# The end of an attention stage: score memory closed a round earlier, feed-forward loads issued from there, products regrouped

## The chip, the cores and the metric

The kernel runs on one core of a Trainium2 chip. The metric is the device time of one execution in microseconds (us), as the median over runs. Lower is better. The core has five engines that each work through their own list of instructions in order and wait for one another by semaphores: TensorE (PE, matmuls; PEld is its weight load), VectorE (DVE), ScalarE (ACT), GpSimd (POOL) and SyncE (SP), which here only issues transfers (DMA).

## The reference

Two stages follow each other: attention with a logarithmic position bias, and a feed-forward network with softplus.

```python
# attention: B, H, S, D = 4, 8, 576, 64
scores = scale * np.matmul(q, k.transpose(0, 1, 3, 2))
scores = scores + bias.transpose(2, 0, 1)[None, :, :, :]
scores = scores - np.max(scores, axis=-1, keepdims=True)
attn = np.exp(scores)
attn = attn / (np.sum(attn, axis=-1, keepdims=True) + 1e-09)
attn_out = np.matmul(attn, v)
# feed-forward: 2304 tokens, d_model 512, d_ff 2048
x = np.ascontiguousarray(attn_out.transpose(0, 2, 1, 3)).reshape(B * S, H * D)
h = x @ w_in
g = np.maximum(h, 0.0) + np.log1p(np.exp(-np.abs(h)))
return (g @ w_out).astype(np.float32)
```

Inputs of the weights are 64-bit floats, which the kernel turns into 32-bit ones with integer operations (`bits`, five steps, the tokens B below) and stores in device memory (`w_d`).

## The kernel before

Attention goes in 16 rounds, n = 0 to 15, each for one batch and one pair of heads. The order of the work in a round is written out by hand as a string of tokens; `emit` turns each into instructions, and each engine keeps the order in which its instructions are emitted. In round n the scores of round n+1 are made beside the second half of round n:

- S, A, X: a score tile of round n+1: its matmuls (line 336), the addition of the bias with the row's extreme (354, DVE), and the exponential (372, ACT).
- T*jc*/buffer: transposes (401) of three tiles of probabilities into a buffer of PSUM (`s0`, `s1`, `t` as 0, 1, 2, or the free half of the output's own memory, `o`); V*jc*/a or /d: the copy out of it into `pt` on ACT (305) or DVE (307). The buffer is free for the next T after its V.
- P0 to P4: the product of `pt` with the values (460), five column blocks that accumulate into `o`. P3 and P4 of round n stand in round n+1.
- I, R, C, G: the reciprocal of the row sums (498, 499), its transpose, the copy and its transfer out (514, 515), and the broadcast loads `rb` (521). O: `o` times `rb` gives `x` (480), which frees `o`; Y: four transfers of `x` to `x_d` (486 to 489).
- B0 to B4, W: `bits` of one weight tile and the store to `w_d` (695).
- D: transposes of the identity matrix whose result nobody reads (629).

Round 15 has no scores to make. Before it the memory for scores (`es_s`: q, k, the bias tiles and, in PSUM, `s0` and `s1`) is closed (line 958) and the pools of the feed-forward stage take its place, among them four PSUM banks for `h`. SP's list then gets three loads of `x` and two of weights (960 to 962). Transposes of round 15 use `t` and `o` alone. The tokens f0 to f12 (`FIRST`) put the first work of the feed-forward stage between them: `wl` loads a weight tile, `xl` loads `x`; `w` (741 on ACT, 743 on POOL or DVE) and `x` (759 on ACT, 760 on DVE) split a tile into a rounded part and the remainder, and `step`.

`step(i)` (line 908) emits, for one visit (512 tokens by 128 of d_ff): `emit_h` (772, 12 matmuls), the softplus of the visit before (`emit_g`, 788 to 804), the splitting of the weights of the visit after (`w_fin`), and `emit_y` (830) of the visit three before. There are 80 visits. Step 0 and 1 are emitted inside round 15, those from 2 on behind it.

```python
 958             es_s.close()
 959             open_ffn()
 960             x_load(0, range(3))
 961             w_load(0, 0)
 962             w_load(1, 0)
```

Of the kernel before, what the change touches and what calls it, by code (L numbers as in the profile page):

```python
# [9 lines left out]
F32 = mybir.dt.float32  # L10
# [6 lines left out]
PSUM = bass.MemoryType.PSUM  # L17
# [11 lines left out]
SH = S // 2  # L29
# [15 lines left out]
ROUND = """  # L45
# [2 lines left out]
G S7/0 S6/2 L4 A8 V20/a T22/1 T11/2 V41/a b V31/d T30/0 B2 A7 b X3 V11/a V22/a b P0 V30/d A5 A6 L1  # L48
X7 P1 X8 B3 X6 X5 L2 P2 T32/0 V32/d L3 B4 W
"""  # L50
STEADY = range(2, 15)
SETS = ((2, 4), (3, 8), (7, 5, 6), (1, 0))

ROUND0 = """
# [6 lines left out]
ROUND1 = """  # L61
# [3 lines left out]
X6 L3 P2 B4 X5 L2  # L65
"""

ROUND15 = """
P3 T00/2 D4 I P4 V00/a T02/2 D4 V02/a T10/2 D6 O R/o V10/a C T01/o V01/d T32/2 V32/d T11/o T12/2 f2 V11/a
V12/a T22/o V22/d f4 P0 T21/2 f3 V21/a f0 P1 T20/2 V20/a f7 T30/2 V30/a T40/2 f8 f1 V40/a f9 B0  # L70
f11 T41/2 P2 B1 f5 f10 V41/a f6 T31/2 B2 B3 f12 V31/a B4
"""
ROUND16 = """
P3 P4 O
"""

FIRST = (
    ('x', 0, 1), ('wl', 0, 1), ('w', 0, 0, True), ('x', 0, 0), ('xl', 0, (3,)), ('wl', 2, 0),
    ('wl', 1, 1), ('x', 0, 2), ('w', 1, 0, True), ('x', 0, 3), ('w', 0, 1, True), ('step', 0), ('step', 1),
)  # L80
FIRST_STEP = 2

PLACE = (0, 1, 2, 3, 4, 7, 8, 5, 6)
# [32 lines left out]
def tile_log_bias_attention__then__softplus_ffn(  # L116
# [13 lines left out]
    nc = tc.nc  # L130
# [9 lines left out]
    def pool(es, name, bufs, side="left", space=SB):  # L140
        return es.enter_context(
            tc.tile_pool(name=name, bufs=bufs, side=side, space=space, reuse_waits="tile")
        )

    const = ctx.enter_context(tc.tile_pool(name="const", bufs=1))
    ident = const.tile([128, 128], F32, name="ident")
# [6 lines left out]
    es_s = ctx.enter_context(ExitStack())  # L153
    nat = pool(es_s, "nat", NAT, "right")
    bp = pool(es_s, "bp", 18, "right")
    ps_s = pool(es_s, "ps_s", 1, "right", PSUM)
    s_buf = [ps_s.tile([128, 2, 512], F32, name=f"s{i}") for i in range(2)]

    es_p = ctx.enter_context(ExitStack())
# [95 lines left out]
    N = 16  # L255
# [123 lines left out]
    def tail(n, i):  # L379

        assert all(("e", n, t) in done for t in TAILS[i])
        done.add(("l", n, i))
        tl = pp.tile([128, 2, 64], F32, tag="tl", name="tl", bufs=9)
        if i < 4:
            src = pairs.pop((n, i))[:, :, 512:S]
        else:
            src = prob[n, 4][:, 512:S].rearrange("p (o c) -> p o c", o=1)
            src = src.to_broadcast([128, 2, 64])
        nc.gpsimd.tensor_copy(tl, src)
        tails[n, i] = tl.rearrange("p a c -> p (a c)")  # L390

    s_use, s_held = [0], set()
    spare = {}

    def turn(blocks, on=None):
        ps = ps_o if on == "o" else s_buf[int(on)]
# [171 lines left out]
    def emit(n, tok):  # L568

        tok, _, on = tok.partition("/")  # L570
        on = (on,) if on else ()
        kind, late_ = tok.rstrip("0123456789"), tok[len(tok.rstrip("0123456789")):]
        a = [int(c) for c in late_]

        def stage(key, make, i, *arg):
            if key not in units:
                units[key] = make(*key[1:])
            units[key][i](*arg)

        if kind in ("S", "A", "X"):  # L580
            if n + 1 < N:
                stage(("s", n + 1, *a), u_s, "SAX".index(kind), *on)
        elif kind in ("Z", "ZA", "ZX"):
            stage(("s", n, *a), u_s, ("Z", "ZA", "ZX").index(kind))
        elif kind == "L":
            if n + 1 < N:
                tail(n + 1, *a)
        elif kind == "ZL":
            tail(n, *a)
        elif kind in ("T", "V"):  # L590
            stage(("t", n, *a), u_t, "TV".index(kind), *on)
        elif kind == "P":
            stage(("p", n - (a[0] >= PV_LATE), *a), u_pv, 0)
        elif kind == "I":
            inv(n)
        elif kind in ("R", "C"):
            stage(("r", n), u_r, "RC".index(kind), *on)
        elif kind == "O":
            if n:
                stage(("x", n - 1), u_x, 0)  # L600
                if n not in STEADY:
                    defer(8, lambda: stage(("x", n - 1), u_x, 1))
        elif kind == "B":
            if 1 <= n <= len(pre):
                stage(("b", n - 1), u_bits, *a)
                if a[0] == 4 and n not in STEADY:
                    defer(8, lambda: stage(("b", n - 1), u_bits, 5))
        elif kind in ("k", "q"):
            emit_load(n + 3, kind)
        elif kind == "v":  # L610
            emit_load_v(n + 2)
        elif kind == "w":
            pre_load(n)
        elif kind == "b":
            if tiles:
                emit_bias(*tiles.pop(0))
        elif kind == "G":
            units["r", n][2]()
        elif kind == "Y":
            stage(("x", n - 1), u_x, 1)  # L620
        elif kind == "W":
            if 1 <= n <= len(pre):
                stage(("b", n - 1), u_bits, 5)
        elif kind == "D":
            if n == N - 1 and "h" not in spare:
                spare["h"] = fp["h"].tile([128, 512], F32, tag="h", name="h")
            to = spare["h"][:, 0:128] if n == N - 1 else ps_o[:, 0, SH:SH + 128]
            for _ in range(a[0]):
                nc.tensor.transpose(to, ident, ident)
        elif kind == "f":  # L630
            w, *arg = FIRST[int(late_)]
            FFN[w](*arg)
        else:
            assert False, tok
# [3 lines left out]
    def defer(k, f):  # L638
        waiting.append([k, f])
# [45 lines left out]
    pre = PRE  # L685
# [3 lines left out]
    def pre_load(i):  # L689
        if i < len(pre):  # L690
            raws[i] = load_raw(dec, *pre[i])
# [6 lines left out]
    es_f = ctx.enter_context(ExitStack())  # L698
    fp = {}

    def open_ffn():
        for nm, bufs in (("raw2", 4), ("xr", 3), ("x0", 4), ("ew", 2), ("gp", 2), ("wr", 1)):
            fp[nm] = pool(es_f, nm, bufs, "right")
        fp["h"] = pool(es_f, "ps_h", 4, "right", PSUM)

    NF = DFF // 128
    wi, wo, wraw = {}, {}, {}
# [2 lines left out]
    def w_load(f, i):  # L710
        if (f, i) in slot:
            a = fp["raw2"].tile([128, 512], F32, tag="a", name="a")
            nc.sync.dma_start(out=a, in_=w_d[slot[f, i]])
        else:
            a = load_raw(fp["raw"], f, i)
        wraw[f, i] = a
# [31 lines left out]
    def x_load(bi, cs=range(4)):  # L748
        t0, nb = blocks[bi]
        for c in cs:  # L750
            a = fp["xr"].tile([128, 512], F32, tag="xr", name="xr")
            nc.sync.dma_start(out=a[:, :nb], in_=x_d[c, :, t0:t0 + nb])
            xraw[bi, c] = a
# [9 lines left out]
    hs, gs, ys = {}, {}, {}  # L763
    def emit_h(bi, f):
        nb = blocks[bi][1]
        ps = spare.pop("h", None)
        if ps is None:
            ps = fp["h"].tile([128, 512], F32, tag="h", name="h")
        i = 0
        for c in range(4):  # L770
            for a, x_ in ((0, 0), (0, 1), (1, 0)):
                nc.tensor.matmul(  # L772
                    ps[:, :nb],
                    lhsT=wi[f][:, a, 128 * c:128 * c + 128],
                    rhs=xs[bi, c][:, x_, :nb],
                    start=(i == 0),
                    stop=(i == 11),
                )
                i += 1
        hs[bi, f] = ps  # L780
# [105 lines left out]
    ps_t, ps_o = (ps_a.tile([128, 2, 512], F32, name=nm) for nm in ("t", "o"))  # L886
# [66 lines left out]
        "step": step,  # L953
    }
    for n in range(N + 1):
        if n == N - 1:
            assert not s_held
            es_s.close()
            open_ffn()
            x_load(0, range(3))  # L960
            w_load(0, 0)
            w_load(1, 0)
        tiles = [(n // B + 1 + (n % B == 3), t) for t in SETS[n % B]]
        if n < 3:
            tiles = [(1, t) for t in ((), range(5), range(5, 9))[n]]
        if n == 1:
            assert not s_held
            s_use[0] = 0
        toks = {0: ROUND0, 1: ROUND1, N - 1: ROUND15, N: ROUND16}.get(n, ROUND).split()
        for i, tok in enumerate(toks):  # L970
            load = {0: LOADS0, 1: LOADS}.get(n, LOADS if n > N - 2 else {}).get(i)
            if load in ("k", "q"):
                emit_load(n + 3, load)
            elif load == "v":
                emit_load_v(n + 2)
            elif load == "v1":
# [93 lines left out]
```

## Time and profile before

| | us |
|---|---|
| median of 3 runs | 685.0 (683.39 to 686.06) |
| the profiled execution, its own time | 685.62 |
| its span, first to last instruction | 683.8 |
| PE busy in the span | 648.1 (95%) |
| ACT, DVE busy | 513.8 (75%), 497.2 (73%) |
| chain that ended last: PE's share | 88% |

In the page, the second part shows busy tenths in 40 slices of 17.1 us. From the seventh slice to the 39th PE stands at 9, except for a 7 in the 16th (256 to 274 us), and in the 16th and 17th PEclk reads 8: that is the end of attention. The windows of the trace, which give each engine's busy time and the granted TensorE clock in any stretch (1.00 is 2.4 GHz, 0.50 is 1.2 GHz), show the place closely. The timeline by engine lists what ran when, with the idle time ahead of it and what ended that in square brackets; the chain gives the steps that set the end.

### The profile page before, as it was taken

What the parts mean: (1) busy time and instruction counts of PE and PEld (TensorE: products, weight loads), DVE (VectorE), ACT (ScalarE), POOL (GpSimd) and SP (SyncE); (2) the same over time, 40 slices, a digit from 0 to 9 for tenths busy, and PEclk for the clock granted to TensorE, in tenths of its full rate; (3) what the DMA queues carried; (4) which work ended last, traced back from release to release, by engine and by line L of the source; (5) the groups of instructions that cost most, each with busy time, mean ns of one, the idle gap of its engine ahead of it and who ended that gap; (6) DMA issues with size and microseconds to landing.
All of it is one profiled execution on the core that took longest, in us unless ns stands there. A gap on an engine that the chain in (4) does not pass through costs nothing.

```text
span 683.8 us, 13233 instructions
## 1 busy us (share of the span) xinstructions
PE 648.1 (95%) x4821; PEld 482.4 (71%) x4821; DVE 497.2 (73%) x1079; ACT 513.8 (75%) x1061; POOL 37.3 (5%) x106
## 2 busy tenths in 40 slices
PE   5688879999999997999999999999999999999997
PEld 2123447667666674678888888888888888888886
DVE  6996558999999994589696874696775565555564
ACT  5899659999999994778686776786676665665654
POOL 0000111111111111100000000000000000000000
PEclk9999989999999998899999999999999999999999
DMA  4986938889788634462240303320300221302220
GB/s 141 310 287 210 343 119 275 265 249 291 247 270 269 196 124 137 131 193 87 99 147 32 115 9 109 107 93 32 106 19 0 108 78 67 119 0 85 70 93 32
DMA packets 51041, 96.85 MB, mean 142 GB/s; under 512 B 7440, under 2 KB 19104, under 8 KB 50976
## 3 DMA queue, kind: packets, MB, share of 16 engines
q1 hardware_dynamic: 50208, 95.34, 42.2%
q8 instruction: 38, 0.62, 0.4%
q10 hardware_dynamic: 768, 0.66, 0.3%
q14 instruction: 27, 0.22, 0.1%
HBM read 67.98 MB, written 28.01 MB: 140 GB/s over the span
## 4 chain that ended last, share of the span: by engine, by line
PE 88%; ACT 5%; DMA 4%; DVE 1%; issue 1%; SPq 1%; ACTq 0%; DVEq 0%
PE y L830 29%; PE h L772 28%; PE o L460 11%; PE s L336 6%; PE s L401 4%; PE t L336 3%; PE acc L225 3%; PE t L401 2%; DMA e_d<-e 2%; ACT e L246 1%; ACT p L372 1%; PE o L401 1%; PE o L336 1%; DMA rb<-r_d 1%; DMA dist<-in_c_dist_dram 1%
## 5 line engine op out<-in xcount | busy, mean ns | idle before, releaser
L772 PE MATMUL h<-x,wi 128*128 128x512 f32 (+1 forms) x960 | 213.8, 372 | 0.3 <-DVE wi L743 0.3
L830 PE MATMUL y<-wo,g 128*128 128x512 f32 x864 | 209.8, 391 | 0.0
L772 PEld LDWEIGHTS h<-x,wi 128*128 128x128 f32 x960 | 170.4, 190 | 33.9 <-DVE wi L743 0.7
L830 PEld LDWEIGHTS y<-wo,g 128*128 128x128 f32 x864 | 161.2, 188 | 33.7 <-DVE g L804 0.2
L795 DVE SCALAR_TENSOR_TENSOR u<-u,e 128x512 f32<-128x512 f32 (+1 forms) x80 | 50.9, 637 | 105.4 <-ACT l L792 105.0
L372 ACT ACTIVATE p<-p,m 128x576 f32<-128x576 f32 x144 | 110.4, 769 | 5.4 <-DVE m L354 1.8
L788 ACT ACTIVATE e<-h 128x512 f32<-128x512 f32 (+1 forms) x80 | 44.3, 553 | 76.7 <-PE h L772 76.7
L460 PE MATMUL o<-pt,vn 128*64 128x256 f32 (+3 forms) x640 | 85.4, 427 | 0.8 <-DVE pt L307 0.7
L354 DVE CUSTOM_DVE_ANT_0 p<-s,b 128x576 f32<-128x576 f32 x79 | 58.4, 753 | 8.5 <-ACT e L246 3.4
L802 ACT ACTIVATE g<-l 128x512 fp32r<-128x512 f32 (+1 forms) x80 | 46.8, 585 | 20.2 <-DVE l L799 10.6
L336 PE MATMUL s<-kn,qn 64*128 64x288 f32 (+1 forms) x416 | 58.6, 415 | 0.2 <-ACT p L347 0.2
L460 PEld LDWEIGHTS o<-pt,vn 128*64 128x64 f32 (+1 forms) x640 | 37.9, 139 | 29.3 <-issue 9.5
L804 DVE TENSOR_TENSOR g<-l,g 128x512 fp32r<-128x512 f32 (+1 forms) x80 | 50.3, 628 | 3.7 <-ACT g L802 3.7
L225 PE MATMUL acc<-m,coef 128*32 128x512 f32 (+17 forms) x352 | 35.5, 502 | 16.4 <-ACT e L246 8.6
L799 DVE TENSOR_TENSOR l<-l,u 128x512 f32<-128x512 f32 (+1 forms) x80 | 50.4, 630 | 0.0
L797 DVE SCALAR_TENSOR_TENSOR l<-h,l 128x512 f32<-128x512 f32 (+1 forms) x80 | 50.4, 630 | 0.0
L792 ACT ACTIVATE l<-u 128x512 f32<-128x512 f32 (+1 forms) x80 | 47.1, 589 | 2.9
L789 ACT ACTIVATE e<-e 128x512 f32<-128x512 f32 (+1 forms) x80 | 47.2, 590 | 2.6
L791 ACT ACTIVATE u<-e 128x512 f32<-128x512 f32 (+1 forms) x80 | 47.2, 590 | 2.5
L305 ACT ACTIVATE pt<-s 128x384 f32<-128x384 f32 x88 | 42.0, 484 | 6.3 <-ACT r L514 4.5
L212 DVE TENSOR_SCALAR m<-lw,pb 128x576 f32<-128x576 f32 (+17 forms) x122 | 44.2, 445 | 0.0
L401 PEld LDWEIGHTS s<-ident,p 64*128 64x128 f32 x624 | 30.7, 142 | 15.6 <-DVE m L354 6.4
(73 smaller groups left out, 692.3 us busy)
## 6 DMA issues: line engine op xcount, KB each, us to landing
e_d<-e SPq DMA_DIRECT2D x36, 295.5 KB, 3.4
qn<-in_q_dram SPq DMA_DIRECT2D x16, 576.0 KB, 6.4
b<-e_d SPq DMA_DIRECT2D x32, 288.0 KB, 3.9
r<-in_moe_w_in_dram SPq DMA_DIRECT2D x16, 512.0 KB, 3.8
r<-in_moe_w_out_dram SPq DMA_DIRECT2D x16, 512.0 KB, 4.3
xr<-x_d SPq DMA_DIRECT2D x28, 256.0 KB, 4.0
vn<-in_v_dram SPq DMA_DIRECT2D x16, 320.0 KB
kn<-in_k_dram SPq DMA_DIRECT2D x16, 288.0 KB, 6.6
```

What stands on the lines that cost most here:

```text
L225: nc.tensor.matmul(acc[32 * g:32 * g + 32, lo:hi], lhsT=coef.rearrange("p o h -> p (o h)"), rhs=hid[s, g][:, lo:hi], start=True, stop=True ...
L336: nc.tensor.matmul(ps[at:at + w, half, :SH], lhsT=q_n[n][rows, hd, c0:c0 + w], rhs=k_n[n][rows, hd], start=True, stop=True, tile_position= ...
L354: nc.vector.tensor_tensor_reduce(prob[n, t].rearrange("p (a c) -> p a c", a=2), st_["ps"], bias[pr, t].rearrange("p (a c) -> p a c", a=2), ...
L372: nc.scalar.activation(p, p, AF.Exp, bias=st_["m"], scale=-1.0, accum_out=ssum[n][:, PLACE.index(t):PLACE.index(t) + 1],)
L401: nc.tensor.transpose(ps[:, a, i], src[rows], ident[rows, 64 * a:64 * a + 64], tile_position=(64 * a, 0))
L460: nc.tensor.matmul(o[up, half, 0:w], lhsT=v_n[n][rows, jb, hd], rhs=pt[n, jb][rows, c0:c0 + w], start=(jb == 0), stop=(jb == 4), tile_posi ...
L772: nc.tensor.matmul(ps[:, :nb], lhsT=wi[f][:, a, 128 * c:128 * c + 128], rhs=xs[bi, c][:, x_, :nb], start=(i == 0), stop=(i == 11),)
L795: nc.vector.scalar_tensor_tensor(u, u, -1.0, e, op0=ALU.add, op1=ALU.subtract)
L797: nc.vector.scalar_tensor_tensor(l, ps, 0.0, l, op0=ALU.max, op1=ALU.add)
L799: nc.vector.tensor_tensor(l, l, u, op=ALU.subtract)
L804: nc.vector.tensor_tensor(g[:, 1], l, g[:, 0], op=ALU.subtract)
L830: nc.tensor.matmul(y, lhsT=g[:, a, 128 * ts:128 * ts + 128], rhs=wo[f][:, w_], start=(first and i == 0), stop=(last and i == 2),)
```

## The change

The memory for scores is closed in two parts. Its SBUF part (q, k, bias) closes inside round 14, by a new token E behind the last bias addition (A6), and the feed-forward pools open there; `h`'s PSUM pool no longer does. Tokens f0 to f2 right behind E load weight tile 0, all four parts of `x` (a pool with four buffers now) and weight tile 1. The buffers `s0` and `s1` stay open until a new token F in round 16, and `h` opens there. Round 15 thus transposes into three buffers, has no D, keeps P3 and P4 of round 14 together and P0, P1, P2 together, and does its roundings (f6 to f11: `w` of tile 0, `x` four times, `w` of tile 1) behind most copies. Round 16 does P3, P4, then step 0, the last O, and step 1. The store of the weight bits of round 14 (W) moves behind the new loads. The tables' rows are cut.

```diff
-STEADY = range(2, 15)
+STEADY = range(2, 17)
+ROUND14 = """
...
+G S7/0 S6/2 L4 A8 V20/a T22/1 T11/2 V41/a b V31/d T30/0 B2 A7 b X3 V11/a V22/a b P0 V30/d A5 A6 E f0
+f1 f2 L1 X7 P1 X8 B3 X6 X5 L2 P2 T32/0 V32/d L3 B4
+"""
 ROUND16 = """
-P3 P4 O
+P3 P4 F f13 O Y B1 B2 B3 B4 f14 W1
 """
 FIRST = (
-    ('x', 0, 1), ('wl', 0, 1), ('w', 0, 0, True), ('x', 0, 0), ('xl', 0, (3,)), ('wl', 2, 0),
...
+    ('wl', 0, 0), ('xl', 0), ('wl', 1, 0), ('wl', 0, 1), ('wl', 2, 0), ('wl', 1, 1),
+    ('w', 0, 0, True), ('x', 0, 0), ('x', 0, 1), ('x', 0, 2), ('x', 0, 3), ('w', 1, 0, True), ('w', 0, 1, True),
+    ('step', 0), ('step', 1),
 )
@@
-    ps_s = pool(es_s, "ps_s", 1, "right", PSUM)
+    es_u = ctx.enter_context(ExitStack())
+    ps_s = pool(es_u, "ps_s", 1, "right", PSUM)
@@
         elif kind == "B":
-            if 1 <= n <= len(pre):
-                stage(("b", n - 1), u_bits, *a)
+            i = min(n, N - 1) - 1
+            if 0 <= i < len(pre):
+                stage(("b", i), u_bits, *a)
@@
         elif kind == "W":
-            if 1 <= n <= len(pre):
-                stage(("b", n - 1), u_bits, 5)
+            i = n - 1 - (a[0] if a else 0)
+            if 0 <= i < len(pre):
+                stage(("b", i), u_bits, 5)
@@
+        elif kind == "E":
+            assert not s_held
+            es_s.close()
+            open_ffn()
+        elif kind == "F":
+            es_u.close()
+            fp["h"] = pool(es_f, "ps_h", 4, "right", PSUM)
@@
-        for nm, bufs in (("raw2", 4), ("xr", 3), ("x0", 4), ("ew", 2), ("gp", 2), ("wr", 1)):
+        for nm, bufs in (("raw2", 4), ("xr", 4), ("x0", 4), ("ew", 2), ("gp", 2), ("wr", 1)):
@@
-        if n == N - 1:
-            assert not s_held
-            es_s.close()
-            open_ffn()
-            x_load(0, range(3))
-            w_load(0, 0)
-            w_load(1, 0)
@@
-        toks = {0: ROUND0, 1: ROUND1, N - 1: ROUND15, N: ROUND16}.get(n, ROUND).split()
+        toks = {0: ROUND0, 1: ROUND1, N - 2: ROUND14, N - 1: ROUND15, N: ROUND16}.get(n, ROUND).split()
```

SP's list at the change of rounds 14 and 15, before (`a` is a weight tile's buffer, `xr` one of `x`; the first three of the rows behind the store are `x`):

```order
L695 DMA w_d_61<-a_3996 128x512
L752 DMA xr_4208<-x_d_59 128x512
L752 DMA xr_4210<-x_d_59 128x512
L752 DMA xr_4212<-x_d_59 128x512
L713 DMA a_4214<-w_d_61 128x512
L713 DMA a_4216<-w_d_61 128x512
L486 DMA x_d_59<-x_4265 128x256
L487 DMA x_d_59<-x_4265 64x320
L488 DMA x_d_59<-x_4265 64x256
L489 DMA x_d_59<-x_4265 64x64
L752 DMA xr_4318<-x_d_59 128x512
```

The same place of SP's list now:

```order
L727 DMA a_4176<-w_d_61 128x512
L766 DMA xr_4178<-x_d_59 128x512
L766 DMA xr_4180<-x_d_59 128x512
L766 DMA xr_4182<-x_d_59 128x512
L766 DMA xr_4184<-x_d_59 128x512
L727 DMA a_4186<-w_d_61 128x512
L710 DMA w_d_61<-a_3996 128x512
L727 DMA a_4276<-w_d_61 128x512
L495 DMA x_d_59<-x_4284 128x256
L496 DMA x_d_59<-x_4284 64x320
L497 DMA x_d_59<-x_4284 64x256
L498 DMA x_d_59<-x_4284 64x64
```

The six loads moved ahead of the store, and the first weight tile ahead of `x`.

ACT's list in round 15, before, from the copy of the row sums on (`wi0`, `wi1` are the weight tiles' rounded parts):

```order
L514 ACTIVATE r_4271<-o_876 9x128
L515 DMA r_d_60<-r_4271 9x128
L741 ACTIVATE wi0_4305<-a_4214 128x512
L305 ACTIVATE pt_4252<-o_876 128x2x3x64
L305 ACTIVATE pt_4252<-t_875 128x2x3x64
L759 ACTIVATE x_4330<-xr_4208 128x512
L305 ACTIVATE pt_4310<-t_875 128x2x3x64
L759 ACTIVATE x_4334<-xr_4210 128x512
L305 ACTIVATE pt_4310<-t_875 128x2x3x64
L759 ACTIVATE x_4348<-xr_4212 128x512
L305 ACTIVATE pt_4281<-t_875 128x2x3x64
L741 ACTIVATE wi1_4367<-a_4216 128x512
```

ACT's list in round 15 now, from behind the same copy and its transfer:

```order
L315 ACTIVATE pt_4224<-s0_82 128x2x3x64
L315 ACTIVATE pt_4215<-s1_83 128x2x3x64
L315 ACTIVATE pt_4231<-t_875 128x2x3x64
L315 ACTIVATE pt_4314<-s1_83 128x2x3x64
L315 ACTIVATE pt_4314<-t_875 128x2x3x64
L755 ACTIVATE wi0_4340<-a_4176 128x512
L773 ACTIVATE x_4343<-xr_4178 128x512
L773 ACTIVATE x_4350<-xr_4180 128x512
L773 ACTIVATE x_4353<-xr_4182 128x512
L773 ACTIVATE x_4360<-xr_4184 128x512
L755 ACTIVATE wi1_4363<-a_4186 128x512
L315 ACTIVATE pt_4366<-s1_83 128x2x2x64
```

The roundings that stood between the copies now stand in one piece behind five of them and ahead of one.

PE's list at the first `h`, before (`tl` are the last 64 columns of the probabilities, T40 and T41):

```order
L401 MATMUL t_875<-ident_66,tl_4104 128x64 x2
L401 MATMUL t_875<-ident_66,tl_4156 128x64 x2
L772 MATMUL h_4229<-x_4330,wi0_4305 128x512 x3
L772 MATMUL h_4229<-x_4334,wi0_4305 128x512 x3
L772 MATMUL h_4229<-x_4348,wi0_4305 128x512 x3
L772 MATMUL h_4229<-x_4373,wi0_4305 128x512 x3
L401 MATMUL t_875<-ident_66,tl_4116 128x64 x2
L401 MATMUL t_875<-ident_66,tl_4167 128x64 x2
L401 MATMUL t_875<-ident_66,tl_4180 128x64 x2
L460 MATMUL o_876<-pt_4310,vn_3804 64x256 x2
L460 MATMUL o_876<-pt_4310,vn_3804 64x320 x2
```

PE's list at the same place now:

```order
L410 MATMUL s1_83<-ident_66,tl_4104 128x64 x2
L410 MATMUL s1_83<-ident_66,tl_4188 128x64 x2
L410 MATMUL s0_82<-ident_66,tl_4116 128x64 x2
L410 MATMUL s0_82<-ident_66,tl_4199 128x64 x2
L410 MATMUL s0_82<-ident_66,tl_4212 128x64 x2
L469 MATMUL o_876<-pt_4314,vn_3804 64x256 x2
L469 MATMUL o_876<-pt_4314,vn_3804 64x320 x2
L469 MATMUL o_876<-pt_4366,vn_3804 64x256 x2
L469 MATMUL o_876<-pt_4366,vn_3804 64x320 x2
L784 MATMUL h_4397<-x_4343,wi0_4340 128x512 x3
L784 MATMUL h_4397<-x_4350,wi0_4340 128x512 x3
```

All transposes and products of attention now stand ahead of the first `h`.

## Rows read from the trace of the kernel before

**Rows 1.** Windows: stretch, its length, each engine's busy us, granted clock, DMA share

```profile
259.40:268.30 8.90, 7.44 (x82) 4.46 (x80) 3.60 (x9) 3.10 (x8) 0.54 (x2) 1.00 0.65 190
268.30:275.20 6.90, 4.57 (x26) 2.33 (x28) 1.35 (x3) 2.92 (x6) 1.27 (x1) 0.51 0.33 106
275.20:278.60 3.40, 2.14 (x23) 1.34 (x20) 1.19 (x2) 2.56 (x6) 0.49 (x1) 1.00 0.70 239
278.60:282.00 3.40, 3.40 (x10) 2.65 (x9) 2.49 (x3) 1.42 (x3) 2.87 (x3) 0.50 0.30 80
282.00:295.40 13.40, 13.14 (x76) 8.70 (x75) 9.38 (x17) 11.55 (x21) 0.00 (x0) 1.00 0.45 139
295.40:683.80 388.40, 384.81 (x1776) 320.31 (x1775) 260.85 (x461) 264.51 (x469) 0.00 (x0) 1.00 0.22 76
```

**Rows 2.** Timeline of PE: start, duration, what, idle time before and its releaser

```profile
256.29 3.13 PE L460 MATMUL o<-pt,vn 128*64 128x256 f32 x24
...
262.44 0.77 PE L460 MATMUL o<-pt,vn 64*64 64x256 f32 x8
...
269.91 0.58 PE L401 MATMUL o<-ident,p 64*128 64x64 f32 x6 [2.03 <-ACT pt L305]
271.22 2.19 PE L460 MATMUL o<-pt,vn 128*64 128x256 f32 x8 [0.72 <-DVE pt L307]
...
287.20 1.89 PE L460 MATMUL o<-pt,vn 128*64 128x256 f32 x16
...
292.80 2.59 PE L772 MATMUL h<-x,wi 128*128 128x512 f32 x10 [0.26 <-DVE wi L743]
295.23 1.09 PE L830 MATMUL y<-wo,g 128*128 128x512 f32 x4
```

**Rows 3.** Timeline of SP's queue at the change of rounds 14 and 15

```profile
255.58 1.82 SPq L521 DMA_DIRECT2D rb<-r_d  x3
260.98 0.33 SPq L695 DMA_DIRECT2D w_d<-a  x1
261.40 2.47 SPq L752 DMA_DIRECT2D xr<-x_d  x3
263.92 0.91 SPq L713 DMA_DIRECT2D a<-w_d  x2
```

**Rows 4.** Timeline of ACT in rounds 14 and 15 and the first steps

```profile
260.57 0.19 ACT L372 ACTIVATION_READ_ACCUMULATOR p<-p,m 128x1 f32 x1
...
268.85 0.63 ACT L741 ACTIVATE wi<-a 128x512 fp32r<-128x512 f32 x1 [3.01 <-DMA a<-w_d]
269.39 0.47 ACT L305 ACTIVATE pt<-o 128x384 f32<-128x384 f32 x1
269.76 0.48 ACT L305 ACTIVATE pt<-t 128x384 f32<-128x384 f32 x1
...
283.30 0.59 ACT L788 ACTIVATE e<-h 128x512 f32<-128x512 f32 x1
...
287.31 0.60 ACT L788 ACTIVATE e<-h 128x512 f32<-128x512 f32 x1
```

**Rows 5.** Timeline of DVE at the same places

```profile
258.33 0.76 DVE L354 CUSTOM_DVE_ANT_0 p<-t,b 128x576 f32<-128x576 f32 x1
...
261.06 0.21 DVE L499 RECIPROCAL ss<-ss 128x9 f32<-128x9 f32 x1
263.25 0.82 DVE L480 TENSOR_TENSOR x<-o,rb 128x256 f32<-128x256 f32 x2 [1.97 <-PE o L460]
...
287.12 0.68 DVE L743 TENSOR_TENSOR wi<-a,wi 128x512 fp32r<-128x512 f32 x1
...
292.06 0.68 DVE L743 TENSOR_TENSOR wi<-a,wi 128x512 fp32r<-128x512 f32 x1
```

**Rows 6.** Windows of the transposes alone (line 401), at attention's start; granted clock fourth

```profile
70.00:73.15 3.15, 2.73 (x46) 0.56 0.93 339
...
73.80:76.00 2.20, 0.40 (x6) 1.00 1.04 390
```

More of the change, by code (lines that the diff above doesn't have):

```diff
@@ L66 @@
 """
+ROUND14 = """
+T10/2 I T00/1 S2/2 S1/1 V10/a B0 S0/0 w T21/0 R/2 A1 C v P3 P4 q A0 V00/a S4/1 A2 B1 X1 k X0 O T40/1
+S3/2 T12/o V21/a A4 V40/d X2 T01/2 Y T02/0 S8/o S5/1 V02/a V01/d b T41/0 T20/1 V12/a X4 T31/o L0 A3
+G S7/0 S6/2 L4 A8 V20/a T22/1 T11/2 V41/a b V31/d T30/0 B2 A7 b X3 V11/a V22/a b P0 V30/d A5 A6 E f0
+f1 f2 L1 X7 P1 X8 B3 X6 X5 L2 P2 T32/0 V32/d L3 B4
+"""
 ROUND15 = """
-P3 T00/2 D4 I P4 V00/a T02/2 D4 V02/a T10/2 D6 O R/o V10/a C T01/o V01/d T32/2 V32/d T11/o T12/2 f2 V11/a
-V12/a T22/o V22/d f4 P0 T21/2 f3 V21/a f0 P1 T20/2 V20/a f7 T30/2 V30/a T40/2 f8 f1 V40/a f9 B0
-f11 T41/2 P2 B1 f5 f10 V41/a f6 T31/2 B2 B3 f12 V31/a B4
+T10/2 I T00/1 T21/0 V10/a V00/d R/2 V21/a C T20/1 V20/d P3 P4 T01/0 V01/a W1 T02/2 V02/d f3 T11/1 O
+V11/a Y T12/0 V12/d T22/2 V22/a G f4 f5 T30/1 V30/a T31/0 V31/d T32/2 V32/a P0 f6 f7 P1 f8 f9 P2 f10
+f11 T40/1 V40/a T41/0 V41/d B0 f12
 """
 ROUND16 = """
-P3 P4 O
+P3 P4 F f13 O Y B1 B2 B3 B4 f14 W1
 """
 FIRST = (
-    ('x', 0, 1), ('wl', 0, 1), ('w', 0, 0, True), ('x', 0, 0), ('xl', 0, (3,)), ('wl', 2, 0),
-    ('wl', 1, 1), ('x', 0, 2), ('w', 1, 0, True), ('x', 0, 3), ('w', 0, 1, True), ('step', 0), ('step', 1),
+    ('wl', 0, 0), ('xl', 0), ('wl', 1, 0), ('wl', 0, 1), ('wl', 2, 0), ('wl', 1, 1),
+    ('w', 0, 0, True), ('x', 0, 0), ('x', 0, 1), ('x', 0, 2), ('x', 0, 3), ('w', 1, 0, True), ('w', 0, 1, True),
+    ('step', 0), ('step', 1),
 )
@@ L392, in tile_log_bias_attention__then__softplus_ffn @@
     s_use, s_held = [0], set()
-    spare = {}
     def turn(blocks, on=None):
@@ L621, in emit @@
         elif kind == "W":
-            if 1 <= n <= len(pre):
-                stage(("b", n - 1), u_bits, 5)
+            i = n - 1 - (a[0] if a else 0)
+            if 0 <= i < len(pre):
+                stage(("b", i), u_bits, 5)
         elif kind == "D":
-            if n == N - 1 and "h" not in spare:
-                spare["h"] = fp["h"].tile([128, 512], F32, tag="h", name="h")
-            to = spare["h"][:, 0:128] if n == N - 1 else ps_o[:, 0, SH:SH + 128]
             for _ in range(a[0]):
-                nc.tensor.transpose(to, ident, ident)
+                nc.tensor.transpose(ps_o[:, 0, SH:SH + 128], ident, ident)
+        elif kind == "E":
[5 more added lines that the diff above has]
+            fp["h"] = pool(es_f, "ps_h", 4, "right", PSUM)
         elif kind == "f":
@@ L701, in open_ffn @@
     def open_ffn():
-        for nm, bufs in (("raw2", 4), ("xr", 3), ("x0", 4), ("ew", 2), ("gp", 2), ("wr", 1)):
+        for nm, bufs in (("raw2", 4), ("xr", 4), ("x0", 4), ("ew", 2), ("gp", 2), ("wr", 1)):
             fp[nm] = pool(es_f, nm, bufs, "right")
-        fp["h"] = pool(es_f, "ps_h", 4, "right", PSUM)
     NF = DFF // 128
@@ L765, in emit_h @@
         nb = blocks[bi][1]
-        ps = spare.pop("h", None)
-        if ps is None:
-            ps = fp["h"].tile([128, 512], F32, tag="h", name="h")
+        ps = fp["h"].tile([128, 512], F32, tag="h", name="h")
         i = 0
```

## The prediction

> **What bounds the kernel now.** I read the windows first. From 295.40 us to the end PE is busy 384.81 of 388.40 us at full clock [rows 1]: that is the feed-forward stage, bound by PE, and the change touches nothing in it. Its 1776 matmuls, 192 of them half as wide, make 1680 full ones, so one costs 388.40 / 1680 = 0.231 us and an `h` of twelve 2.77 us. What can move is the stretch from 259.40, when round 14's P0 to P2 end [rows 2], to the first `y` at 295.23 [rows 2]. Since all behind it is the same work without idle time, each us by which that first `y` comes earlier is a us of the total.
>
> The stretch takes 35.8 us. Its work at full clock: seven products (P3, P4 of round 14, all five of round 15), where three in 3.13 us make 1.04 for a P0 to P3, and 0.77 for a P4 [rows 2], so 5 x 1.04 + 2 x 0.8 = 6.8; some 14 transposes at 0.2, 2.8 (six matmuls each, 46 in 2.73 us at about half clock [rows 6], so 0.36 there and 0.18 at full); four `h`, 11.1. That is 20.7 us. The other 15 are idle time and half clock: the clock stands at about 0.5 in 268.30 to 275.20 and again in 278.60 to 282.00, and PE is busy 7.44 of 8.90 us ahead of the first, 2.14 of 3.40 ahead of the second [rows 1].
>
> Then the timelines, for what stops PE. ACT is free of exponentials at 260.76 [rows 4]. SP's five loads stand behind the store of weight bits, which goes at 260.98, and behind three `x` loads; the first weight tile is issued at 263.92 [rows 3], and ACT, in order, waits 3.01 us for it, to 268.85 [rows 4]. The copies of round 15 that stand behind it wait too, and with them the transposes (PE idle 2.03 us for ACT at 269.91 [rows 2]). The clock has fallen by then, and a P costs 2.19 in place of 1.04 [rows 2].
>
> **The change, part by part.**
>
> *The loads.* f0 to f2 stand behind round 14's `rb`, whose issue ends at 255.58 + 1.82 = 257.40 [rows 3]. They wait for score memory, at the latest for the last bias addition of round 14, which ends at 259.1 [rows 5]. So tile 0 is issued at 257.5 to 259.2, against 263.92. From issue to use it took 268.85 - 263.92 = 4.93 us [rows 3, 4], so it is there at 262.4 to 264.1; `x` and tile 1 need 2.47 us for three loads [rows 3], so they follow within 3 us. ACT will want tile 0 at 266.9 (below): the wait of 3.01 goes, hidden by some 3 us of copies. The store behind them is needed only several steps later. P3, P4 and O of round 14 don't move past any load that they need.
>
> *Round 15.* I walk it with the durations of before. The reciprocal ends at 261.27 [rows 5]. V00 on DVE (0.5, as the ACT copies of 0.47 [rows 4]) frees `s1` for T20 at 261.9. P3 and P4 of round 14 come behind T20, where before P3 was the first thing: 262.25 to 264.05. Eight transposes follow, which share three buffers with five copies on ACT, one each 0.37 us [rows 4], and three on DVE, with O's 0.82 [rows 5] among them; the slowest string, T01, V01, T12, V12 behind V02 and O, T31, T32, has the last T at 266.8. P0 to P2: 3 x 1.04, to 270.0. T40, T41: 270.5. P3 and P4 in 1.89 [rows 2]: 272.4. Beside that ACT does its six roundings from 266.9 on, 0.54 each, to 270.1, then V40, to 271.0, ahead of P4 at 271.6: hidden, by 0.6 us.
>
> *The first steps.* `h`(0) ends at 272.4 + 2.77 + 0.1 = 275.3. Now a new wait: `h`(2) needs weight tile 2, which step 1 splits behind the softplus of `h`(0). From that softplus's start to the end of the split it took 287.12 + 0.68 - 283.30 = 4.50 us [rows 4, 5]. So tile 2 is ready at 279.9, while `h`(1) has ended at 278.0: PE is idle 1.9 us. Step 2's softplus began 4.01 us behind step 1's [rows 4], of which 0.47 was a copy of attention that is now earlier: 3.54, so 278.9. Tile 3 was ready 292.06 + 0.68 - 287.31 = 5.43 us behind that [rows 4, 5]; round 15's O, 0.82, lay in DVE's way and is now earlier, so I take 5.1: 284.0. From there to the first `y` 295.23 - 292.74 = 2.49 [rows 2, 5]: 286.5.
>
> *D.* Fourteen transposes of the identity go; they cost PE some 2 us in which it had nothing else to do. What is late when they are gone is the clock, below.
>
> *The sum.* 295.23 - 286.5 = 8.7 us, all at full clock. What the clock takes back is not in the trace of before, since the order of PE's work is new. The quiet times are 259.7 to 262.25 and 264.0 to 266.8, with transposes in both, and PE's two waits at 278.0 and about 282. Before, the clock fell after stretches of that kind [rows 1]. Nothing lost is one end. The other is P0 to P2 all at half clock, 3 x (2.19 - 1.04) = 3.5 us [rows 2]; a fall at `h`(2) costs less, as that wait has slack behind it. A gain is excluded: I walk at full clock. I take one product's worth, 1.15, nearer to the lower end, because P3 and P4 stand between the two quiet times, and the first fall of before came with a wait of 3 us that is gone. That leaves 7.5 us.
>
> The profiled execution took 685.62 us, 1.8 outside its span; 685.62 - 7.5 = 678.1. The median of three is 0.6 lower than that execution, so 677.5.
>
> **A rule weighed.** At attention's start, PE did transposes for 2.73 of 3.15 us at a clock of 0.56, and from 73.80 on the clock is full [rows 6]; little else than transposes had run since 70. The Trainium skill says otherwise ("TensorE: Matmul & The Clock Gate", Part 4: PE-mode transpose): a transpose in transpose mode doesn't count as busy for the clock. Here the trace disagrees, if these are such transposes. By that rule the quiet times of the new round 15 would hold nothing that keeps the clock up, the removed D did nothing either, and the sum would be 4.5 in place of 7.5 (rival 1).
>
> **The rivals.**
>
> 1. *The transposes don't hold the clock.* Then it falls in the first quiet time and P3 and P4 of round 14 and P0 to P2 of round 15 run at half: 3.5 us, and some 1.7 for the first two, of which the buffers' string hides about 1: 8.7 - 4.2 = 4.5 us gained, 680.5. For it: both falls of before had transposes as PE's main work ahead [rows 1, 2]. Against it: [rows 6]. This is the case that the skill's rule above would give.
>
> 2. *The loads don't come earlier in use.* If the early loads wait for memory or land slowly, tile 0 is there at 268.85 as before. ACT's six roundings then end at 272.1, V40 at 272.6, P4 starts 1.5 us later, and with `x` later still 2.7: 679.0 to 680.2. For it: transfers took 4.93 us. Against: nothing that f0 could wait for is issued later than 259.
>
> 3. *Slower: the clock stays low from P0 to the first `y`.* With D gone and new waits ahead of `h`(2) and `h`(3), PE never gets back to full. Then P0 to P4, the transposes and `h`(0) cost 8.3 us more (`h`(0) ends at 283.6), and `h`(1) to `h`(3) at 5.5 each bring the first `y` to 300.2, 5.0 us later than before: 690. It is slower than before from the point on where the low clock lasts into `h`(3). Against it: in both stretches of before the clock rose again under dense products or one `h` [rows 1, 2], and the new order has over 10 us of dense work from P0 to `h`(1).
>
> 4. *It doesn't do what it says.* If the end of the stage were set by the chain of the softplus alone, earlier loads would be swallowed. The walk has this chain in it; it costs 1.9 and some 1.5 us of waits, and those are counted.
>
> **How the numbers follow.** A difference within 0.5% (3.4 us) is about what a measurement of this kernel can tell from no change. The forecast, 677.5, with 0 to 2.3 us lost to the clock, 676.3 to 678.7: 0.68. Rival 1, 680.5: 0.13. Rival 2, 679.0 to 680.2: 0.09. Both together, 682 to 684, which is no difference: 0.04. Rival 3: 0.03. Better than the walk, below 675.5: 0.03. The range 675.0 to 680.6 takes in the forecast's, rival 2 and most of rival 1, with half a us for the runs' spread; what it leaves out is about 0.2. Faster by over 0.5%: 0.68 + 0.13 + 0.09 + 0.03 = 0.93; within: 0.04; slower: 0.03.
>
> **What would show it.** The loads: SP's first weight load at 257.5 to 259.2, and no wait of ACT for a transfer in round 15. Round 15: P0 at 267, P4 at 271.6, the first `h` at 272.4. The new wait: PE idle near 2 us ahead of `h`(2), released by DVE's split, and less ahead of `h`(3). The first `y` at 286.5 to 288.7. The clock: at most one stretch at half, of a few us, between 262 and 284. Wrong would be: a second and third stretch at half; `x` that lands behind 268; a wait of V40 behind roundings that delays P4; a feed-forward stage of other than 388 us behind the first `y`.

## The result

The changed kernel takes 677.57 us as median of four runs (677.19 to 678.86), the kernel before 685.53 (683.39 to 686.27); the ratio is 0.989, with a 95% interval of 0.985 to 0.993. The forecast was 677.5, the range 675.0 to 680.6. Later, on chip 7, the same pair stood at 681.52 and 686.78, ratio 0.993 (0.9905 to 0.9957): 5.3 us in place of 8.0. Both lie in what the prediction called faster, but the total hit the forecast more closely than its terms did, as will be seen.

The profiled execution has a span of 675.5 us (683.8 before). Its windows, with the columns of [rows 1], over the stretch that the change is about and cut at the first `h` (272.40 here) and the idle time behind the second (278):

```profile
259.40:264.10 4.70, 3.83 (x58) 2.30 (x58) 2.32 (x8) 1.86 (x5) 0.54 (x2) 1.00 0.74 264
264.10:272.40 8.30, 6.52 (x72) 3.50 (x68) 6.14 (x8) 5.85 (x12) 4.36 (x3) 1.00 0.43 144
272.40:278.00 5.60, 5.60 (x29) 4.43 (x24) 2.54 (x5) 2.18 (x4) 0.77 (x2) 1.00 0.46 136
278.00:287.00 9.00, 7.04 (x27) 4.54 (x26) 7.90 (x13) 8.81 (x17) 0.00 (x0) 1.00 0.46 143
```

The granted clock is 1.00 all through; before it was about half for 10 us [rows 1]. SP's queue and ACT, which answer to [rows 3] and to ACT's wait in [rows 4]:

```profile
255.21 0.58 SPq L727 DMA_DIRECT2D a<-w_d  x1
255.84 1.85 SPq L766 DMA_DIRECT2D xr<-x_d  x4
257.74 0.43 SPq L727 DMA_DIRECT2D a<-w_d  x1
259.59 0.32 SPq L710 DMA_DIRECT2D w_d<-a  x1
```

```profile
266.03 0.62 ACT L755 ACTIVATE wi<-a 128x512 fp32r<-128x512 f32 x1
266.55 2.18 ACT L773 ACTIVATE x<-xr 128x512 fp32r<-128x512 f32 x4
```

Tile 0 is issued 8.7 us earlier than before (7.3 when both are counted from round 15's reciprocal, see below) and ahead of the store, and ACT's rounding of it shows no wait. PE, which answers to [rows 2]:

```profile
265.53 3.13 PE L469 MATMUL o<-pt,vn 128*64 128x256 f32 x24
...
271.98 0.76 PE L469 MATMUL o<-pt,vn 64*64 64x256 f32 x6 [1.17 <-DVE pt L317]
272.67 5.74 PE L784 MATMUL h<-x,wi 128*128 128x512 f32 x24
278.89 0.73 PE L784 MATMUL h<-x,wi 128*128 128x512 f32 x2 [0.48 <-ACT wi L755]
280.30 3.37 PE L784 MATMUL h<-x,wi 128*128 128x512 f32 x12 [0.67 <-DVE wi L757]
284.42 2.59 PE L784 MATMUL h<-x,wi 128*128 128x512 f32 x10 [0.75 <-DVE wi L757]
286.84 2.89 PE L842 MATMUL y<-wo,g 128*128 128x512 f32 x12
```

P0 to P2 run as one block at full clock, the two new waits ahead of `h`(2) and `h`(3) are there, and so is a wait of 1.17 us inside P4, ahead of its last six matmuls, where the prediction had none. DVE, with what answers to [rows 5]:

```profile
259.68 0.21 DVE L508 RECIPROCAL ss<-ss 128x9 f32<-128x9 f32 x1
...
267.20 4.26 DVE L774 TENSOR_TENSOR x<-xr,x 128x512 fp32r<-128x512 f32 x4 [1.18 <-ACT x L773]
271.38 0.54 DVE L317 COPY pt<-s 128x384 f32<-128x384 f32 x1
```

V41, the copy that P4 waits for, stands behind the four remainders of `x`, and these took 4.26 us. The walk of the prediction had no term for them; in the kernel before, one of them by itself took 0.68:

```profile
271.08 0.68 DVE L760 TENSOR_TENSOR x<-xr,x 128x512 fp32r<-128x512 f32 x1
```

**A measure inside one execution.** Executions of one kernel reach round 15 at different times: its reciprocal starts at 261.06 us in the first profile of the kernel before and at 262.65 in a second one, at 259.68 and 262.44 in two of the changed kernel. The change touches nothing ahead of round 14's loads, and from round 14's P0 to the reciprocal both kernels take the same, 4.77 and 4.78 us. From the reciprocal's start to the first `y`, which I call the stage, it is 295.23 - 261.06 = 34.17 before and 286.84 - 259.68 = 27.16 now; behind the first `y` both take the same, 388.57 and 388.66. So the change is worth 7.0 us here, and 1.4 of the 8.3 between the two spans came from ahead of it, where the two programs do the same. All experiments are read by the stage, and by their time against runs of the kernel before on the same chip.

### The profile page after: what moved, and what is told of

Read it like the earlier page. It is cut to its first block, busy times and chain, and to the rows that moved or that the text cites. A ratio compares the mean times of both kernels' runs of the same rounds, so it can differ in the third digit from the quotient of the medians.

```text
span 675.5 us, 13207 instructions
## 1 busy us (share of the span) xinstructions
PE 642.0 (95%) x4807; PEld 478.2 (71%) x4807; DVE 499.2 (74%) x1082; ACT 512.2 (76%) x1058; POOL 38.0 (6%) x106
## 4 chain that ended last, share of the span: by engine, by line
PE 89%; ACT 5%; DMA 3%; DVE 2%; issue 1%; ACTq 1%; SPq 0%; DVEq 0%
PE y L842 29%; PE h L784 29%; PE o L469 10%; PE s L346 6%; PE s L410 4%; PE acc L235 4%; PE t L346 3%; ACT p L382 2%; PE t L410 1%; ACT e L256 1%; DMA e_d<-e 1%; PE o L346 1%; PE o L410 1%; DMA dist<-in_c_dist_dram 1%; ACTq L530 0%
## 5 line engine op out<-in xcount | busy, mean ns | idle before, releaser
L469 PE MATMUL o<-pt,vn 128*64 128x256 f32 (+3 forms) x640 | 82.9, 419 | 1.2 <-DVE pt L317 1.2
L235 PE MATMUL acc<-m,coef 128*32 128x512 f32 (+17 forms) x352 | 36.9, 521 | 16.1 <-ACT e L256 8.6
L315 ACT ACTIVATE pt<-s 128x384 f32<-128x384 f32 (+1 forms) x93 | 44.2, 483 | 8.4 <-ACT r L523 4.5
L410 PEld LDWEIGHTS s<-ident,p 64*128 64x128 f32 x672 | 32.5, 140 | 18.4 <-DVE m L364 6.7
```

The lines of the kernel that those rows point to most:

```text
L235: nc.tensor.matmul(acc[32 * g:32 * g + 32, lo:hi], lhsT=coef.rearrange("p o h -> p (o h)"), rhs=hid[s, g][:, lo:hi], start=True, stop=True ...
L410: nc.tensor.transpose(ps[:, a, i], src[rows], ident[rows, 64 * a:64 * a + 64], tile_position=(64 * a, 0))
L469: nc.tensor.matmul(o[up, half, 0:w], lhsT=v_n[n][rows, jb, hd], rhs=pt[n, jb][rows, c0:c0 + w], start=(jb == 0), stop=(jb == 4), tile_posi ...
```

## The experiments

**Both kernels once more.** First the changed kernel itself.

> The changed kernel itself, unchanged, as the measure for the others of this call and for a second look at the clock. From the end of round 15's sums (start of the reciprocal on DVE) to the first y it took 27.2 us in its first profile, 34.2 in the kernel before, 25.4 with the tail copies early. Theory: again 27 to 27.5 us with no stretch at half clock, or 1.5 to 2 us more with one; total 7 to 9 us below the kernel before on the same chip. If the gain were a matter of the chip or of chance, it would be 28.5 or more without any stretch at half clock.

Its stage is 289.61 - 262.44 = 27.17 us, to 0.01 the first one, without a stretch at half clock. The total gain is 5.3 us, below the 7 to 9 that I had expected. Then the kernel before.

> The kernel before, unchanged, for a second look at its end of attention: from the start of round 15's reciprocal to the first y it took 34.2 us in its first profile, with two stretches at half clock (6.8 and 3.4 us). Theory (the late weight tile makes the first of them, whatever the execution): the wait of ACT for it is 2.5 to 3.5 us again, at least one stretch at half clock follows it, and the stage takes 32.5 to 34.5 us. If the clock fell by chance in the first profile only, it would be 31.5 us or less.

```profile
270.11 0.63 ACT L741 ACTIVATE wi<-a 128x512 fp32r<-128x512 f32 x1 [2.69 <-DMA a<-w_d]
```

```profile
272.00:274.00 2.00, 1.70 (x10) 0.72 0.09 12
274.00:276.00 2.00, 2.00 (x14) 0.50 0.70 217
280.00:282.00 2.00, 2.00 (x6) 0.50 0.18 51
```

The rows are ACT's wait and windows of PE (stretch, length, PE busy, granted clock, DMA share). Wait and two stretches at half clock are there again; the stage is 296.06 - 262.65 = 33.41 us. By the stage the change is worth 6.2 to 7.0 us, and both totals, 8.0 and 5.3, fit that with the differences of 1.6 to 2.8 us that executions of one kernel show ahead of it.

**The loads alone, the order alone.** The change has two halves that can be had apart.

```diff
# loads alone: the kernel before, and in it
+X3 V11/a V22/a b P0 V30/d A5 A6 E L1 ...          (round 14)
+        elif kind == "E":
+            es_s.close(); open_ffn()
+            w_load(0, 0); x_load(0); w_load(1, 0)
...
# order alone: the changed kernel, and in it
-... A5 A6 E f0 f1 f2 L1 ... L3 B4                 (round 14)
+... A5 A6 L1 ... L3 B4 W
-T10/2 I T00/1 ...                                 (round 15)
+E f1 f0 f2 T10/2 I T00/1 ...
```

> The kernel before with one part of the change alone: the SBUF part of the score memory closes in round 14 and tile 0, the four parts of x and tile 1 are loaded there; round 15 keeps its old order, its two transposing buffers and D (only the load of the fourth part of x moves with the others). Theory A (the late weight tile was the root: ACT waited 3.01 us for it, and the clock fell behind that wait): the wait is gone, and with it most of the two stretches at half clock, so 3.0 to 6.5 us less than before, 679 to 682.5 us. Theory B (the order carries the gain; transposes into two buffers between roundings were slow by themselves): at most 1.5 us less than before, 684 or more, and the clock falls as before.

> The changed kernel with the other part alone: closing and loads stand at the start of round 15, behind the store of round 14's weight bits, x ahead of tile 0, as in the kernel before; order, buffers and roundings of the changed kernel. Theory A (loads are the root): ACT waits again, now at the first rounding behind five copies, about 2 us; V40 and P4 come 1.5 to 2.7 us later than in the changed kernel, 679 to 680.3 us. Theory B (the order carries it all): within 0.7 us of the changed kernel, 677 to 678.3. If the loads were everything, it would be near the time before, 683 or more.

Loads alone took 684.25 us against 686.67 of the kernel before (ratio 0.9948, 0.9914 to 0.9982), order alone 682.9 (0.9945, 0.9919 to 0.9970). Both totals missed their forecasts, which had been counted from the first result. The stages: 294.54 - 264.35 = 30.19 and 291.16 - 261.69 = 29.47 us. Neither half carries it all; together they gave 27.2. With the loads alone ACT's wait is 0.35 us, but PE still stops for the copies of two buffers, and the clock falls once:

```profile
269.47 0.63 ACT L755 ACTIVATE wi<-a 128x512 fp32r<-128x512 f32 x1 [0.35 <-DMA x_d<-x]
```

```profile
272.00:274.00 2.00, 1.59 (x8) 0.57 0.53 153
274.00:276.00 2.00, 2.00 (x16) 0.57 0.96 333
```

So theory A in its strong form, that the late weight tile was the root of both stretches at half clock, is wrong: its removal takes one of them and 4.0 us of the stage (3.2 against the second profile of the kernel before). With the order alone ACT's wait for tile 0 is 0.61 us, not 2, and what it costs shows elsewhere: P4 waits 1.76 us in place of 1.17, PE is busy 0.29 of 2 us, and the clock falls at the first `h`, where 24 matmuls then take 7.37 us in place of 5.74:

```profile
268.76 0.63 ACT L755 ACTIVATE wi<-a 128x512 fp32r<-128x512 f32 x1 [0.61 <-DMA a<-w_d]
```

```profile
274.71 0.76 PE L469 MATMUL o<-pt,vn 64*64 64x256 f32 x6 [1.76 <-DVE pt L317]
275.40 7.37 PE L784 MATMUL h<-x,wi 128*128 128x512 f32 x24
```

```profile
273.00:275.00 2.00, 0.29 (x4) 1.00 0.84 255
275.00:277.00 2.00, 2.00 (x11) 0.72 0.65 160
277.00:279.00 2.00, 2.00 (x6) 0.50 0.60 189
```

Of the 2.3 us that it loses against the whole change, 7.37 - 5.74 = 1.6 is the clock and 1.76 - 1.17 = 0.6 the wait.

**The wait ahead of P4.** Two ways to take it away: put V41 ahead of the remainders, or make the remainders short.

```diff
# tail copies early
-... V32/a P0 f6 f7 P1 f8 f9 P2 f10 f11 T40/1 V40/a T41/0 V41/d B0 f12
+... V32/a T40/1 V40/a P0 T41/0 V41/d f6 f7 P1 f8 f9 P2 f10 f11 B0 f12
...
# weight splits early
-... V21/a C T20/1 ... P0 f6 f7 P1 f8 f9 P2 f10 f11 T40/1 ...
+... V21/a C f6 f11 T20/1 ... P0 f7 P1 f8 f9 P2 f10 T40/1 ...
```

> The changed kernel with T40, V40, T41, V41 ahead of the roundings, so that V41 on DVE stands ahead of the four remainders of x. In the changed kernel these took 4.26 us for four where 0.60 apart was expected, V41 came behind them, and PE waited 1.17 us for it ahead of P4. Theory C (V41 behind the stretched remainders is what made the last stage late): P4 follows P3 at once, the first h starts 1.2 to 1.9 us earlier, 675.6 to 676.4 us. Rival D (the first h needs the same remainders and waits for them instead): at most 0.4 us less, 677.1 or more.

```profile
269.72 4.04 DVE L774 TENSOR_TENSOR x<-xr,x 128x512 fp32r<-128x512 f32 x4
```

```profile
269.14 3.83 PE L469 MATMUL o<-pt,vn 128*64 128x256 f32 x32
272.90 5.74 PE L784 MATMUL h<-x,wi 128*128 128x512 f32 x24
```

P1 to P4 are one block, the first `h` follows without a wait, and the remainders, though still 4.04 us long, hold nothing up. The stage is 287.08 - 261.71 = 25.37 us, 1.8 less than the changed kernel's: theory C, not D. The total is 679.25 us, ratio 0.9883 (0.9846 to 0.9920) to the kernel before on that chip. The forecast of 675.6 to 676.4 was counted from the first result and wasn't met; the changed kernel wasn't run on that chip, so by the total the edit can't be told from it (0.989 in the first result). Theory C rests on the stage.

> The changed kernel with the splits of tile 0 and 1 (ACT, then 1.28 us each on POOL) right behind the copy of the row sums, where ACT and DVE sit idle; the four x stay where they are. Theory E (POOL's splits, which ran beside DVE's remainders of x, stretched those from 0.6 to 1.07 us): with POOL idle the four take 2.4 to 2.8 us, V41 and P4 come 1.2 us or more earlier, 675.8 to 676.6 us. Rival F (ACT's own writes or the loads stretch them): the four still take about 4.2 us, and the time stays at 677.3 or more.

```profile
270.88 2.50 DVE L774 TENSOR_TENSOR x<-xr,x 128x512 fp32r<-128x512 f32 x4 [0.80 <-ACT x L773]
```

With POOL idle the same four take 2.50 us, 687 ns each against 1122 in the changed kernel, where POOL was busy 2.96 of their 4.26 us: theory E. The mean hides how they were slow. Asked for one at a time, the second and the third remainder of the changed kernel took 0.68 us each; the first and the fourth came while POOL was at a subtraction, and took longer by what was left of it:

```profile
266.74 1.28 POOL L757 TENSOR_TENSOR wi<-a,wi 128x512 fp32r<-128x512 f32 x1 [6.71 <-ACT wi L755]
267.20 1.37 DVE L774 TENSOR_TENSOR x<-xr,x 128x512 fp32r<-128x512 f32 x1 [1.18 <-ACT x L773]
269.32 1.59 POOL L757 TENSOR_TENSOR wi<-a,wi 128x512 fp32r<-128x512 f32 x1 [1.30 <-ACT wi L755]
269.69 1.76 DVE L774 TENSOR_TENSOR x<-xr,x 128x512 fp32r<-128x512 f32 x1
```

Both ended about 0.55 us behind the end of POOL's (268.02 and 270.91). The Trainium skill has the rule for it ("SBUF — State Buffer", "SBUF: two separate sides", in its reading of the port diagram): VectorE with two SBUF inputs and a GpSimd operation that reads SBUF hold one pair of ports in turn, each for its whole instruction. The trace agrees with these four rows. But the time didn't fall: 680.27 us, ratio 0.9902 (0.9864 to 0.9940), stage 290.48 - 262.93 = 27.55. The edit had its own price. Tile 1 hadn't landed when ACT came to it:

```profile
266.71 0.63 ACT L755 ACTIVATE wi<-a 128x512 fp32r<-128x512 f32 x1 [1.86 <-DMA a<-w_d]
```

```profile
267.77 0.40 PE L410 MATMUL s<-ident,p 64*128 64x64 f32 x6 [1.24 <-ACT pt L315]
...
269.73 4.37 PE L469 MATMUL o<-pt,vn 128*64 128x256 f32 x24
```

```profile
267.00:269.00 2.00, 0.89 (x20) 0.97 0.28 92
269.00:271.00 2.00, 2.00 (x18) 0.50 0.34 80
```

The copies behind it came late, PE stopped for 1.24 us, the clock fell, and P0 to P2 took 4.37 us in place of 3.13. Behind that, what the short remainders are worth can be seen:

```profile
274.48 1.89 PE L469 MATMUL o<-pt,vn 128*64 128x256 f32 x16
```

P3 and P4 have no wait, and the first `h` comes only 0.4 us later behind the reciprocal than in the changed kernel (276.30 - 262.93 = 13.37 against 12.99), although P0 began 0.95 us later and P0 to P2 took 1.24 longer: some 1.8 us came back. The loss ahead of it is the kernel before in small: one load that isn't there, on an engine that works in order, and half clock behind it.

**The waits ahead of `h`(2) and `h`(3).** On top of the early tail copies, tiles 2 and 3 are split ahead of step 1's softplus, and tile 1 ahead of `x`.

```diff
-... V41/d f6 f7 P1 f8 f9 P2 f10 f11 B0 f12        (tail copies early)
+... V41/d f6 f11 f7 P1 f8 f9 P2 f10 B0 f12
...
-    ('step', 0), ('step', 1),
+    ('step', 0), ('step', 1), ('w', 2, 0), ('wl', 3, 0),
...
-P3 P4 F f13 O Y B1 B2 B3 B4 f14 W1
+P3 P4 F f16 f13 O Y f15 B1 B2 B3 B4 f14 W1
+    items[0], items[1] = ((1, 1),), ((2, 1),)
...
+    w_fin(3, 0)
     for i in range(FIRST_STEP, len(seq) + 3):
```

> The changed kernel with the tail copies early and, beside that, weight tiles 2 and 3 split ahead of step 1's softplus (tile 1's split ahead of x, tile 3's load ahead of step 0), so that the second and third h after the first have no split to wait for. Theory G (those splits, behind two softplus, are what h(2) and h(3) wait for: 0.48 + 0.67 and 0.75 us in the changed kernel): the waits are gone and the first y comes 2.3 to 3.0 us earlier than with the tail copies alone, 22.4 to 23.1 us behind the reciprocal; total 673 to 675 us on a chip where the changed kernel takes 677.6. Rival H (the first y waits for the softplus of the first h, which moves by no more than the 0.5 us of one split on ACT): 24.6 us or more behind the reciprocal, 0.8 us gained at most.

```profile
271.82 11.26 PE L784 MATMUL h<-x,wi 128*128 128x512 f32 x48
282.93 0.63 PE L842 MATMUL y<-wo,g 128*128 128x512 f32 x2
284.16 2.58 PE L842 MATMUL y<-wo,g 128*128 128x512 f32 x10 [0.61 <-DVE g L816]
286.79 0.74 PE L784 MATMUL h<-x,wi 128*128 128x512 f32 x2
288.28 2.59 PE L784 MATMUL h<-x,wi 128*128 128x512 f32 x10 [0.75 <-DVE wi L757]
290.71 2.93 PE L842 MATMUL y<-wo,g 128*128 128x512 f32 x12
```

Four `h` run as one block and the first `y` starts 22.3 us behind the reciprocal, as theory G had it. But it stops after two matmuls for the softplus, and `h`(4) then waits 0.75 us as `h`(3) did. The second `y` comes at 290.71 - 260.63 = 30.08; with the tail copies alone at 292.61 - 261.71 = 30.90, in the changed kernel at 292.36 - 259.68 = 32.68. So at the second `y` this edit is 0.8 us ahead, and it doesn't keep that: further on PE stops once more for a split, where with the tail copies alone it hardly does.

```profile
276.08 0.63 ACT L755 ACTIVATE wi<-a 128x512 fp32r<-128x512 f32 x1 [3.20 <-DMA a<-w_d]
306.19 2.59 PE L784 MATMUL h<-x,wi 128*128 128x512 f32 x10 [0.98 <-DVE wi L757]
```

From the reciprocal to the last instruction it takes 675.0 - 260.63 = 414.4 us, with the tail copies alone 676.0 - 261.71 = 414.3, and the changed kernel 415.8 and 415.7 in its two profiles. G was right that the splits are what `h`(2) and `h`(3) wait for, and wrong about the worth, which is nothing at the end. Rival H has the worth, but its reason isn't what happened. The first of the rows shows ACT waiting 3.20 us for the load of tile 3 ahead of the first softplus, which so began 276.61 - 260.63 = 15.98 us behind the reciprocal, 1.7 later than with the tail copies alone (275.96 - 261.71 = 14.25), where H had allowed 0.5. What tile 3 loaded in time would give was not tried. The kernel took 677.05 us, where on the same chip the changed kernel took 681.52 and the kernel before 686.78: ratio 0.987 (0.984 to 0.990) to the latter. It is below both, but of the 3.1 us between its profiled execution and that of the changed kernel 1.8 lie ahead of the reciprocal (260.63 against 262.44), and the rest is the tail copies' 1.3.

**Do transposes hold the clock?** The rule of the Trainium skill ("TensorE: Matmul & The Clock Gate", Part 4, PE-mode transpose) that was weighed ahead of the result, put to the test by itself: 108 transposes whose result nobody reads, ahead of P0.

```diff
-... T32/2 V32/a P0 f6 f7 ...
+... T32/2 V32/a D9 D9 D9 D9 D9 D9 D9 D9 D9 D9 D9 D9 P0 f6 f7 ...
```

> The changed kernel with 108 more transposes of the identity (token D) ahead of P0 of round 15: a stretch of at least 8 us in which PE does nothing but transposes. Theory I (transposes hold the clock up): full clock all through it, 108 of them at about 0.15 us take 16 us or less, and P0 behind them takes 1.04 us. Theory J (transposes don't count as busy for the clock): it falls to half inside the stretch and is still low at P0, which then takes 2.1 us.

```profile
268.01 12.01 PE L637 MATMUL o<-ident 128*128 128x128 f32 x108
279.95 3.13 PE L469 MATMUL o<-pt,vn 128*64 128x256 f32 x24
```

```profile
268.01:279.95 11.94, 11.94 (x112) 1.00 0.37 106
```

Full clock over 11.94 us of nothing but transposes, and P0 to P2 behind them at full clock: theory I. For transposes as this kernel issues them, the rule doesn't hold. (This is one execution, of 689.84 us, with transposes of 128x128 back to back; for attention's own, which are 64 columns wide and have waits between them, there are the rise of the clock in [rows 6] and the changed round 15, which kept 1.00.)

## Why the prediction was right, and where it wasn't

I set its steps against the changed kernel's first profile, each counted from the start of the reciprocal (261.06 in the walk, 259.68 here).

- *The loads*: forecast 257.5 to 259.2, which is 3.6 to 1.9 us ahead of the reciprocal; measured 255.21, 4.5 ahead. `rb` ahead of them was done at 255.17, and nothing held them. No wait in ACT. Right in kind, with more cover than thought.
- *Round 15 up to P2*: P0 at 5.8 forecast (266.9), 5.85 measured. Three products in 3.13 us. Right.
- *P4*: forecast 10.5; its last six matmuls began at 271.98 - 259.68 = 12.30, and the first `h` at 12.99 in place of 11.3. **This is the term that failed.** The prediction looked for V40 on ACT behind the roundings and found 0.6 us of cover; it did not follow V41 on DVE behind the four remainders, and had no price for remainders beside POOL. V40 itself ended at 9.8, as forecast (9.9). The experiments show both halves: ahead of the remainders V41 costs nothing (25.37 us, against the walk's 286.5 - 261.06 = 25.4), and without POOL they take 2.50 us.
- *The new waits*: from step 1's softplus to tile 2, 4.50 forecast, 279.56 + 0.68 - 275.73 = 4.51 measured; step 2's softplus 3.54 behind step 1's, measured 3.53; tile 3 5.1, measured 5.1; from there to the first `y` 2.49, measured 2.47. Right to a few hundredths.
- *The clock*: 1.15 us taken, none lost in two profiles. It is not a term to be left out, though: two experiments that lengthened PE's wait from 1.17 to 1.76 us, or the one of 0.21 ahead of T12 to 1.24, lost 1.6 and 1.2 us to it.
- *The sum*: 8.7 at full clock less 1.15 was 7.5; measured 7.0 by the first profiles, 6.2 from the second of the kernel before. The error at P4 (1.7 too little) and the clock (1.15 too much) lay on opposite sides, and what lies ahead of round 15 put another 1.4 on the first pair of spans. That 677.5 was met to 0.1 is luck; that the stage gains 6 to 7 us is not.

Of the rivals, the first (transposes don't hold the clock) fell with the clock of 1.00 in the changed round 15 and by its own experiment. The second has its mechanism shown by the order alone, where late loads cost 2.3 us, in the forecast's 1.5 to 2.7, though 1.6 of it by way of the clock. (Its sum holds a slip: V40 at 272.6 against P4 at 271.6 makes 1.0 us, not 1.5.) The third never came near: no experiment on the new order shows more than one stretch at half clock. The fourth, that the softplus chain swallows the gain, did not hold for this change. What lies beyond it was swallowed when tiles 2 and 3 were split early, but there a late load had moved the chain too, so how much the chain by itself would take stays open.

What stays open: why two executions of one kernel reach round 15 up to 2.8 us apart. The profiles show the clock falling at different places in the first 100 us, but whether that is the reason was not tested.

## What to carry to other kernels

Where two stages meet, ask of each engine in order which instruction waits for a load and what stands behind it; moving the load is worth as much as what is queued behind its wait, and moving the order without the load, or the load without the order, gave about two thirds or less of both. When roundings or other side work is collected into one block "behind" the copies, follow every copy that is still behind that block, on each engine apart, and look for a second engine that reads the same memory at the time. Take a gain at the boundary from a marker just ahead of it to one just behind it in the same execution, since totals of several hundred us carry chance of the size of the gain. Then look whether the rest of the execution takes as long as before: the 0.8 us of the last edit were gone some 15 us later.

## What the runs showed of the hardware

- POOL and DVE: four subtractions of 128x512 on DVE took 4.26 us beside POOL's subtractions and 2.50 without them. Those that came while POOL was at one took 1.37 and 1.76 us, the two others 0.68.
- The clock: PE's wait of 1.17 us ahead of P4 cost no clock in two profiles; one of 1.76 us there, and one of 1.24 us between transposes, were followed by a stretch at 0.50.
- Transposes alone kept the granted clock at 1.00 for 11.94 us.
